# Fused attention and soft-MoE kernel: input loads cut in halves and held to a window of three

## The chip, the cores and the metric

The kernel runs on one core of a Trainium2 chip. The metric is the device time of one execution in microseconds (us); the unchanged kernel was timed three times. One further execution was recorded by the hardware profiler, and everything that is read from a profile or a trace below comes from that one. The core has four compute engines with a queue each (PE for matmuls, DVE for vector work, ACT for activations and copies, POOL for further vector work) and SP, whose queue issues all the DMA transfers of this kernel. Each queue runs its instructions in the order in which they were written.

## The reference

All numbers are 32-bit floats. There are 8 batches of 8 heads, 576 positions and 64 features; `phi` has 32 memory slots per position.

```python
a = softmax(phi, axis=slots)                      # (8, 8, 576, 32); max, exp, sum, divide
k_m = einsum('bhsm,bhsd->bhmd', a, k)             # 576 positions pooled into 32 slots
v_m = einsum('bhsm,bhsd->bhmd', a, v)
attn = softmax(q @ k_m^T / 8, axis=slots)         # (8, 8, 576, 32)
x = (attn @ v_m), heads side by side              # (4608, 512)
logits = x @ moe_phi                              # (4608, 32): 8 experts of 4 slots
d = softmax(logits, axis=rows); slot_in = d^T @ x
slot_out[e] = relu(slot_in[e] @ w1[e]) @ w2[e]    # 8 experts, w1 512x1024, w2 1024x512
out = softmax(logits, axis=slots) @ slot_out      # (4608, 512)
```

The column softmax over all 4608 rows needs every batch, so the experts can only start when the last batch is through.

## The kernel before

**Stages.** For each batch `b` the kernel loads `phi`, `k`, `v` and `q`, pools `k` and `v` over positions (`pool_phi`, `pool_kv`), computes the attention (`attend`) and its share of the routing (`route`). The running parts are merged and end in the tile `SIM` (L1095), the input of all experts. Then the 16 MB of `w1` and 16 MB of `w2` are multiplied in pieces of 1 MB (L1159, L1208), and a last loop forms the 36 output blocks (L1319), copies them out of PSUM by turns on ACT and DVE (L1328, L1330) and stores them (L1338).

**What sets the order.** Nothing is issued where it is written. Every step is handed to a planner (`plan.add`) with its engine, an estimated cost, the tiles that it reads and writes and, for a load, an estimated transfer time. `Plan.order` then plays the whole kernel through with these numbers and emits the steps in the order in which they came out, engine by engine. A step can depend on a part of a tile (`split`, `part`). `FILL` steps (L500) are matmuls on a tile of ones whose result is not used; the planner puts them where PE would be idle.

**Loads.** `load` (L480) is one planner step on SP that issues one DMA. The first loads have fixed places (`FIRST`): `phi0 k0 v0 mphi q0 phi1 k1 v1 q1`. A `phi` load has 576 KB; a `k`, `v` or `q` load has 1152 KB, in four blocks (index `c`) of 128 partitions by 576 numbers. The buffers are few: three for `phi`, two for the pair of `k` and `v`, two for `q`. Weight pieces (`load_w`) lie in the same large tile (`arena`) as the buffers of the attention: six pieces have room of their own, and the others take over space that the attention has given up.

**The steps that the prediction follows, for one batch.** DVE L535 takes the maximum over `phi`; PE L543, DVE L548, PE L557 and ACT L568 spread it; POOL L573 subtracts it, in place in the `phi` tile; ACT L579 is the exponential; POOL L586 adds up; PE L596, DVE L603 and L604 make the reciprocal. PE L623 pools `k` and `v`, ACT L639 and L646 scale them, PE L657 and L658 transpose them, ACT L661 copies the result. DVE L702 transposes `q` in two halves (`q_blocks`: half `h` reads the first or the last two of the four blocks). PE L734 forms scores, twice per batch; DVE L748 transposes them, DVE L765 takes the maximum, POOL L770 subtracts, ACT L775 is the exponential, DVE L780 the sum, DVE L789 its reciprocal, POOL L793 the product, DVE L798 transposes back, PE L809 and ACT L814 turn it for the routing.

Of the kernel before, what the change touches and what calls it, by code (L numbers as in the profile page):

```python
# [16 lines left out]
PE, DVE, ACT, POOL, SP = range(5)  # L17
# [3 lines left out]
class Plan:  # L21
# [19 lines left out]
    def add(self, eng, cost, fn, r=(), w=(), also=(), pri=None, dma=0.0, slack=0.0):  # L41
        i = len(self.ops)
        deps = set()
        tiles = set()
        for x in r:
            for key in x:
                tiles.add(key[0])
                if key in self.last_w:
                    deps.add(self.last_w[key])
        for x in w:  # L50
            for key in x:
                tiles.add(key[0])
# [12 lines left out]
        for t in tiles:  # L65
            t.users += 1
        need = tiles + [t for t in also if t not in tiles]
        self.ops.append((eng, cost, fn, deps, i + self.bias if pri is None else pri, dma, tiles, need, slack))
# [159 lines left out]
def dve(n):  # L228
    return 0.15 + n / 960.0
# [51 lines left out]
def kernel(  # L281
# [24 lines left out]
    nc = tc.nc  # L306
    B, H, S, D = q.shape
# [29 lines left out]
    def keep(name, shape, dtype=F32, parts=1):  # L337
        return Tile(ap=const.tile(shape, dtype, name=name), parts=parts)
# [138 lines left out]

    DMA_RATE = 380e3

    def load(dst, src, nbytes, w, pri=None):  # L480
        add(
            SP, 0.06, lambda: nc.sync.dma_start(dst(), src), w=[w],  # L482
            dma=nbytes / DMA_RATE, pri=pri,
        )


    FIRST = ["phi0", "k0", "v0", "mphi", "q0", "phi1", "k1", "v1", "q1"]
# [1 line left out]
    def first(name):  # L489
        return FIRST.index(name) - 1000 if name in FIRST else None  # L490
# [29 lines left out]
    def rows(x, b):  # L520

        return x[b].rearrange("h (p j) y -> (h p) (j y)", j=J).rearrange("(c r) x -> r c x", r=P)


    def pool_phi(b):
# [1 line left out]
        ph = lambda: pt.ap.rearrange("p (c j m) -> p c j m", c=C, j=J)  # L527
        load(
            lambda: pt.ap.rearrange("p (c x) -> p c x", c=C), rows(phi, b), H * S * M * 4, pt,
            pri=first(f"phi{b}"),  # L530
        )
        mx, mh, mb, es, rs = pmxs.tile(), pmhs.tile(), pmbs.tile(), pess.tile(), prss.tile()
        add(
# [74 lines left out]

    def pool_kv(b, pt, ph, rs):

        kb = kvs.tile().split(2)
        kv = lambda: kb.ap.rearrange("p (i c x) -> p i c x", i=2, c=C)
        for i, (src, name) in enumerate(((k, "k"), (v, "v"))):
            load(lambda i=i: kv()[:, i], rows(src, b), H * S * D * 4, kb.part(i), pri=first(f"{name}{b}"))
        acc = b_kv.tile()
        kp, vm = kps.tile(), vms.tile()

# [64 lines left out]


    def load_q(b):
        qt = qs.tile()
        load(
            lambda: qt.ap.rearrange("p (c x) -> p c x", c=C), rows(q, b), H * S * D * 4, qt,
            pri=first(f"q{b}"),
        )
        return qt  # L690

    def at_view(atb):
# [2 lines left out]
    def q_blocks(qt):  # L695

        halves = []
        for h in range(2):
            qT = qTs.tile()

            def f(h=h, qT=qT):
                nc.vector.transpose(  # L702
                    qT.ap.rearrange("p (i u y) -> p u i y", i=2, y=Y),
                    qt.ap[:, h * QT_SZ: h * QT_SZ + QT_SZ].rearrange("p (u i x) -> p u i x", i=2, x=Y),
                )

            add(DVE, dve(QT_SZ), f, r=[qt], w=[qT])
            halves.append(qT)
        return halves

# [664 lines left out]
```

## Time and profile before

| what | value |
|---|---|
| time, median of 3 runs | 220.69 us (218.91 to 223.28) |
| time of the profiled execution | 219.11 us |
| its span in the trace | 217.3 us |
| granted TensorE clock, mean | 0.954 of full speed |
| busy share PE, DVE, ACT, POOL | 85%, 63%, 39%, 41% |
| moved by DMA | 76.52 MB, 352 GB/s over the span |

The span runs from the first to the last instruction in the trace; 1.81 us of the execution lie outside it. The profiled execution was 1.58 us below the median of the three timed runs. A busy PE here is in part PE on `FILL` matmuls: L500 has 41.0 us of its 184.7 us.

### The profile page before, as it was taken

Reading aid. Unit: us, or ns where it says so; the run is one execution under the profiler, and the core shown is the slowest. Engines: PE = TensorE matmul, PEld = TensorE weight load, DVE = VectorE, ACT = ScalarE, POOL = GpSimd, SP = SyncE. Lnnn points to the kernel's source line nnn. Section 1 sums busy time; section 2 is a strip of 40 time slices with the busy share of each in tenths; the row PEclk is TensorE's granted clock in tenths of the full one; section 3 lists DMA queues with packets and bytes.
Section 4 is the critical chain, followed back from the end, with each engine's and each line's share of the span. In section 5 each row is a group of like instructions: output and inputs, shape, how many; then the busy total and the mean of one; then the engine's idle time right before and its main releaser. Section 6 shows DMA issues by size and latency. Waiting matters only on the chain.

```text
span 217.3 us, 6743 instructions
## 1 busy us (share of the span) xinstructions
PE 184.7 (85%) x2934; PEld 119.5 (55%) x2934; DVE 136.4 (63%) x244; ACT 84.0 (39%) x223; POOL 88.8 (41%) x96
## 2 busy tenths in 40 slices
PE   7698888969699989997999999989999799989700
PEld 7596467556466565655756566566543245644500
DVE  3336495978589798896758787459605840278700
ACT  2022406146066283672563855510103322166600
POOL 3380849486568575869294498000000000000000
PEclk9999999988969999998899999999999999999965
DMA  6999999999999999999944987799999999049997
GB/s 219 383 381 387 382 388 380 389 380 383 359 386 372 391 384 388 344 392 412 403 184 140 416 285 324 250 411 411 407 408 409 407 410 364 16 199 416 416 415 291
DMA packets 27885, 76.52 MB, mean 352 GB/s; under 512 B 1744, under 2 KB 5840, under 8 KB 27856
## 3 DMA queue, kind: packets, MB, share of 16 engines
q1 hardware_dynamic: 27856, 76.09, 92.3%
q8 instruction: 23, 0.38, 0.7%
q14 instruction: 6, 0.05, 0.1%
HBM read 66.65 MB, written 9.44 MB: 350 GB/s over the span
## 4 chain that ended last, share of the span: by engine, by line
PE 48%; DMA 17%; DVE 9%; ACT 8%; issue 6%; POOL 4%; SPq 2%; DVEq 1%; ACTq 0%; POOLq 0%
PE scbank L734 9%; DMA arena<-in_moe_w_dram 9%; PE kvbank L623 8%; PE bank L1159 7%; DMA top<-in_q_dram 5%; PE bank L809 3%; PE bank L912 3%; DMA out_dram<-arena 3%; PE bank L829 3%; ACT arena L579 3%; PE bank L500 2%; PE kvbank L1208 2%; SPq L482 2%; PE bank L934 2%; DVE arena L702 2%
## 5 line engine op out<-in xcount | busy, mean ns | idle before, releaser
L500 PE MATMUL bank<-ones 128*128 128x128 f32 x252 | 41.0, 310 | 1.1 <-DVE ones L445 1.1
L500 PEld LDWEIGHTS bank<-ones 128*128 128x128 f32 x252 | 36.6, 220 | 7.0 <-issue 5.7
L586 POOL TENSOR_TENSOR arena<-arena 128x128 f32<-128x128 f32 (+2 forms) x32 | 23.4, 731 | 12.1 <-ACT arena L579 10.2
L702 DVE STREAM_TRANSPOSE arena<-top 128x1152 f32<-128x1152 f32 x16 | 21.7, 1360 | 9.6 <-DMA top<-in_q_dram 9.6
L573 POOL TENSOR_TENSOR arena<-arena 128x1152 f32<-128x1152 f32 x8 | 21.1, 2632 | 15.8 <-ACT arena L568 15.8
L623 PE MATMUL kvbank<-arena 64*32 64x128 f32 x1152 | 21.9, 279 | 3.3 <-ACT arena L579 1.8
L770 POOL TENSOR_TENSOR arena<-arena,smx 128x576 f32<-128x576 f32 x16 | 18.5, 1158 | 13.6 <-DVE smx L765 13.5
L734 PE MATMUL scbank<-arena 32*32 32x288 f32 x512 | 20.9, 407 | 2.3 <-issue 2.0
L623 PEld LDWEIGHTS kvbank<-arena 64*32 64x32 f32 x1152 | 16.6, 107 | 8.0 <-ACT arena L579 3.6
L748 DVE STREAM_TRANSPOSE arena<-scbank 128x576 f32<-128x576 f32 x16 | 12.4, 777 | 11.8 <-PE scbank L734 11.8
L535 DVE TENSOR_REDUCE arena<-arena 128x128 f32<-128x1152 f32 x8 | 17.5, 2186 | 2.9 <-DMA arena<-in_phi_dram 2.9
L814 ACT COPY arena<-bank 96x384 f32<-96x384 f32 x32 | 14.6, 481 | 11.9 <-PE bank L809 11.9
L793 POOL TENSOR_TENSOR arena<-arena,ssm 128x576 f32<-128x576 f32 x16 | 18.3, 1156 | 1.4 <-DVE ssm L789 1.3
L1208 PE MATMUL kvbank<-arena 128*32 128x512 f32 x128 | 16.0, 600 | 2.7 <-DMA arena<-in_moe_w_dram 2.5
L809 PE MATMUL bank<-ident,arena 128*96 128x128 f32 x96 | 16.2, 294 | 0.7 <-DVE arena L886 0.5
L798 DVE STREAM_TRANSPOSE arena<-arena 128x576 f32<-128x576 f32 x16 | 12.1, 758 | 5.1 <-POOL arena L793 5.1
L1159 PE MATMUL bank<-arena,SIM 128*32 128x256 f32 x256 | 14.2, 380 | 0.7 <-DVE SIM L1095 0.7
L1330 DVE COPY arena<-bank 128x512 f32<-128x512 f32 x18 | 12.1, 690 | 3.8 <-PE bank L1319 3.8
L1319 PE MATMUL bank<-sr,cT 128*128 128x512 f32 x36 | 13.3, 470 | 1.4 <-DVE sr L1306 0.3
L809 PEld LDWEIGHTS bank<-ident,arena 128*96 128x96 f32 x96 | 10.3, 134 | 5.7 <-issue 2.9
L734 PEld LDWEIGHTS scbank<-arena 32*32 32x32 f32 x512 | 8.0, 104 | 8.7 <-issue 3.2
L1328 ACT COPY arena<-bank 128x512 f32<-128x512 f32 x18 | 10.5, 587 | 5.4 <-PE bank L1319 5.2
(113 smaller groups left out, 259.0 us busy)
## 6 DMA issues: line engine op xcount, KB each, us to landing
arena<-in_moe_w_dram SPq DMA_DIRECT2D x32, 1024.0 KB, 11.4
arena<-in_k_dram SPq DMA_DIRECT2D x8, 1152.0 KB, 9.8
arena<-in_v_dram SPq DMA_DIRECT2D x8, 1152.0 KB, 12.5
top<-in_q_dram SPq DMA_DIRECT2D x8, 1152.0 KB, 10.8
out_dram<-arena SPq DMA_DIRECT2D x12, 768.0 KB, 6.8
arena<-in_phi_dram SPq DMA_DIRECT2D x8, 576.0 KB, 11.5
arena<-in_moe_phi_dram SPq DMA_DIRECT2D x1, 64.0 KB, 9.0
```

Of the source, the lines that this page charges most:

```text
L500: lambda: nc.tensor.matmul(warm.ap, ones, ones, start=True, stop=True,),
L535: lambda: nc.vector.tensor_reduce(mx.ap, ph().rearrange("p c j m -> p c m j"), axis=AX.X, op=ALU.max),
L573: lambda: nc.gpsimd.tensor_tensor(ph(), ph(), mb.ap.unsqueeze(2).to_broadcast([P, C, J, M]), op=ALU.subtract),
L586: plus = lambda o, x, y: nc.gpsimd.tensor_tensor(o, x, y, op=ALU.add)
L623: nc.tensor.matmul(acc.ap[M * c: M * c + M, a, : 2 * D], ph()[h0: h0 + HALF, c, j, :], kv()[h0: h0 + HALF, :, c, j * D: j * D + D], start= ...
L702: nc.vector.transpose(qT.ap.rearrange("p (i u y) -> p u i y", i=2, y=Y), qt.ap[:, h * QT_SZ: h * QT_SZ + QT_SZ].rearrange("p (u i x) -> p ...
L734: nc.tensor.matmul(scb.ap[M * c: M * c + M, r, :JY], kT.ap[h0: h0 + Y, i * P + M * c: i * P + M * c + M], qT[c // 2].ap.rearrange("p (i c ...
L770: lambda: nc.gpsimd.tensor_tensor(exv(), exv(), bc(mx), op=ALU.subtract),
L793: lambda: nc.gpsimd.tensor_tensor(exv(), exv(), bc(sm), op=ALU.mult),
L809: nc.tensor.transpose(tp.ap[:T, t * P: t * P + P], aT.ap[:, x: x + T], ident)
L1159: nc.tensor.matmul(hb.ap[NS * j: NS * j + NS, :256], SIM.ap[:, 2 * i + c, NS * e: NS * e + NS], wv[:, c, 256 * j: 256 * j + 256], start=(e ...
L1208: nc.tensor.matmul(pacc.ap[NS * x: NS * x + NS, 0, :DM], hT()[:, 4 * t + 2 * i + j, NS * e: NS * e + NS], wv[:, j, t, :], start=(e == 0 an ...
```

## The change

The loads of `k`, `v` and `q` are cut in two halves of two blocks each (576 KB), and the tiles are split so that a reader can wait for the half that it needs: L702 of half `h` now reads only half `h` of `q`, while L623 still reads all of `k` and `v`. All loads of `phi`, `k`, `v` and `q` are marked `fenced`: before such a load, from the fourth on, SP first issues a DMA that copies four bytes out of the tile filled by the third fenced load ahead of it into a small tile `fence`. The queue has to wait until that load has landed before it can issue the copy, and the load stands behind the copy. The loads of `mphi` and of the weights are not fenced.

```diff
-    def load(dst, src, nbytes, w, pri=None):
-        add(
-            SP, 0.06, lambda: nc.sync.dma_start(dst(), src), w=[w],
-            dma=nbytes / DMA_RATE, pri=pri,
-        )
+    DEPTH = 3
+    fence_b = keep("fence", [1, 8])
+    sent = []
+
+    def load(dst, src, nbytes, w, pri=None, rate=DMA_RATE, fenced=False):
+        def f():
+            if fenced:
+                if len(sent) >= DEPTH:
+                    x = sent[-DEPTH]
+                    k = len(sent) % 8
+                    nc.sync.dma_start(fence_b.ap[:, k: k + 1], x)
+                sent.append(dst()[0:1, 0, 0:1])
+            nc.sync.dma_start(dst(), src)
+
+        add(SP, 0.06, f, w=[w], dma=nbytes / rate, pri=pri)
...
-        kb = kvs.tile().split(2)
+        kb = kvs.tile().split(4)
         kv = lambda: kb.ap.rearrange("p (i c x) -> p i c x", i=2, c=C)
         for i, (src, name) in enumerate(((k, "k"), (v, "v"))):
-            load(lambda i=i: kv()[:, i], rows(src, b), H * S * D * 4, kb.part(i), pri=first(f"{name}{b}"))
+            for h in range(2):
+                x = slice(2 * h, 2 * h + 2)
+                load(
+                    lambda i=i, x=x: kv()[:, i, x], rows(src, b)[:, x], H * S * D * 2,
+                    kb.part(2 * i + h), pri=first(f"{name}{b}"), fenced=True,
+                )
...
-            add(DVE, dve(QT_SZ), f, r=[qt], w=[qT])
+            add(DVE, dve(QT_SZ), f, r=[qt.part(h)], w=[qT])
```

`load_q` is cut in the same way, and the load of `phi` is only marked `fenced`. The planner knows of the halves and not of the copies, and it makes a new order for all engines.

On SP the program began with these loads, in order:

```order
L482 DMA arena<-in_phi_dram 128x4x288
L482 DMA arena<-in_k_dram 128x4x576
L482 DMA arena<-in_v_dram 128x4x576
L482 DMA arena<-in_moe_phi_dram 128x4x32
L482 DMA top<-in_q_dram 128x4x576
L482 DMA arena<-in_phi_dram 128x4x288
L482 DMA arena<-in_k_dram 128x4x576
```

and begins so now (line numbers in rows of the changed kernel are its own; L495 is the load, L493 the copy, `top` holds `q`):

```order
L495 DMA arena<-in_phi_dram 128x4x288
L495 DMA arena<-in_k_dram 128x2x576 x2
L493 DMA fence<-arena 1x1
L495 DMA arena<-in_v_dram 128x2x576
L493 DMA fence<-arena 1x1
L495 DMA arena<-in_v_dram 128x2x576
L495 DMA arena<-in_moe_phi_dram 128x4x32
L493 DMA fence<-arena 1x1
L495 DMA top<-in_q_dram 128x2x576
L493 DMA fence<-arena 1x1
L495 DMA top<-in_q_dram 128x2x576
L493 DMA fence<-arena 1x1
```

The first copy reads `phi0` and stands ahead of the first half of `v0`; from there on a copy stands ahead of each input load.

On DVE, between the scores of batch 0 (`scbank`) and the maximum over `phi2`, before:

```order
L748 STREAM_TRANSPOSE arena<-scbank 128x576
L765 TENSOR_REDUCE smx_79<-arena 128x18
L702 STREAM_TRANSPOSE arena<-top 128x18x2x32
L535 TENSOR_REDUCE arena<-arena 128x128
L748 STREAM_TRANSPOSE arena<-scbank 128x576
L548 TENSOR_REDUCE pmh_83<-bank_63 128x2
L765 TENSOR_REDUCE smx_80<-arena 128x18
```

and now (L768 was L748, L785 was L765, L722 was L702, L548 was L535):

```order
L768 STREAM_TRANSPOSE arena<-scbank 128x576
L785 TENSOR_REDUCE smx_79<-arena 128x18
L722 STREAM_TRANSPOSE arena<-top 128x18x2x32
L768 STREAM_TRANSPOSE arena<-scbank 128x576
L785 TENSOR_REDUCE smx_80<-arena 128x18
L548 TENSOR_REDUCE arena<-arena 128x128
```

The transpose and the maximum of the second scores of batch 0 moved ahead of the maximum over `phi2`.

On PE, where the pooling of batch 7 meets the scores of batch 6, before:

```order
L809 MATMUL bank_64<-ident,arena 96x128 x3
L623 MATMUL kvbank<-arena 32x128 x48
L657 MATMUL bank_62<-ident,arena 128x128 x2
L658 MATMUL bank_62<-ident,arena 128x128
L912 MATMUL bank_64<-arena 32x258 x6
L734 MATMUL scbank<-arena 32x288 x16
```

and now (L829 was L809, L675 was L657, L676 was L658, L684 was L666, L932 was L912, L754 was L734, L641 was L623, L513 was L500):

```order
L829 MATMUL bank_64<-ident,arena 96x128 x3
L675 MATMUL bank_63<-ident,arena 128x128 x2
L676 MATMUL bank_63<-ident,arena 128x128
L684 MATMUL bank_62<-mphd,arena 32x64 x4
L513 MATMUL bank_65<-ones 128x128
L932 MATMUL bank_64<-arena 32x258 x6
L754 MATMUL scbank<-arena 32x288 x16
L641 MATMUL kvbank<-arena 32x128 x24
```

The pooling of batch 7 (L623, now L641) moved from ahead of the transposes and scores of batch 6 to behind them.

More of the change, by code (lines that the diff above doesn't have):

```diff
@@ L529, in pool_phi @@
             lambda: pt.ap.rearrange("p (c x) -> p c x", c=C), rows(phi, b), H * S * M * 4, pt,
-            pri=first(f"phi{b}"),
+            pri=first(f"phi{b}"), fenced=True,
         )
@@ L684, in load_q @@
     def load_q(b):
[L685 to L689, printed above, removed]
+        qt = qs.tile().split(2)
+        for h in range(2):
+            x = slice(2 * h, 2 * h + 2)
+            load(
+                lambda x=x: qt.ap.rearrange("p (c x) -> p c x", c=C)[:, x], rows(q, b)[:, x],
+                H * S * D * 2, qt.part(h), pri=first(f"q{b}"), fenced=True,
+            )
         return qt
```

## Prediction

> **What bounds the kernel now.** The page comes first: the size of the span, the engines, the transfers by slice (40 slices of 5.43 us) and the chain that ended last.
>
> ```profile
> span 217.3 us, 6743 instructions
> DVE  3336495978589798896758787459605840278700
> DMA  6999999999999999999944987799999999049997
> GB/s 219 383 381 387 382 388 380 389 380 383 359 386 372 391 384 388 344 392 412 403 184 140 416 285 324 250 411 411 407 408 409 407 410 364 16 199 416 416 415 291
> PE 48%; DMA 17%; DVE 9%; ACT 8%; issue 6%; POOL 4%; SPq 2%; DVEq 1%; ACTq 0%; POOLq 0%
> ```
>
> No engine is full over the whole span, so the kernel has to be read by stages. The transfers run at about 384 GB/s up to 108 us, then drop, then run at about 410 GB/s to 184 us. To see what ends the stages I took the chain of waits in order of time, and what SP's queue waited for between 86 and 146 us.
>
> ```profile
> 145.05 0.30 DVE SIM L1095
> 145.39 7.98 PE bank L1159 x144
> 167.15 18.83 DMA arena<-in_moe_w_dram
> 186.02 1.06 PE kvbank L1208 x8
> SPq L482 <- PE kvbank L623: 27.6, 3, 11.2
> SPq L482 <- DVE SIM L1095: 3.5, 1, 3.5
> ```
>
> The attention ends with `SIM` at 145.05 us. Behind it everything is fixed: the last weight piece lands at 186 us after an unbroken stream, and its earlier pieces waited for room in the arena, which attention steps (L623, L1095) gave up. So the weight stream and the output loop follow the end of the attention, and whatever moves `SIM` moves the end by as much. The question is what the change does to the 145 us of attention. Here are DVE's rows that touch fresh inputs, from its timeline (start, duration, and in brackets the idle time before and who ended it), and the engines' busy time in four stretches (after the length: PE, PEld, DVE, ACT and POOL, then clock, DMA share and GB/s).
>
> ```profile
> 14.42 2.64 DVE L702 STREAM_TRANSPOSE arena<-top 128x1152 f32<-128x1152 f32 x2 [6.39 <-DMA top<-in_q_dram]
> 16.98 2.10 DVE L535 TENSOR_REDUCE arena<-arena 128x128 f32<-128x1152 f32 x1
> 26.16 1.38 DVE L702 STREAM_TRANSPOSE arena<-top 128x1152 f32<-128x1152 f32 x1 [1.26 <-DMA top<-in_q_dram]
> 28.01 2.15 DVE L535 TENSOR_REDUCE arena<-arena 128x128 f32<-128x1152 f32 x1 [0.47 <-DMA arena<-in_phi_dram]
> 37.09 1.38 DVE L702 STREAM_TRANSPOSE arena<-top 128x1152 f32<-128x1152 f32 x1 [1.99 <-DMA top<-in_q_dram]
> 39.05 2.17 DVE L535 TENSOR_REDUCE arena<-arena 128x128 f32<-128x1152 f32 x1
> 50.57 2.26 DVE L535 TENSOR_REDUCE arena<-arena 128x128 f32<-128x1152 f32 x1
> 92.73 2.23 DVE L535 TENSOR_REDUCE arena<-arena 128x128 f32<-128x1152 f32 x1
> 14.40:40.00 25.60, 21.54 (x564) 16.30 (x570) 17.89 (x23) 7.46 (x19) 16.40 (x17) 1.00 1.06 384
> 60.00:80.00 20.00, 18.83 (x360) 12.45 (x365) 17.58 (x31) 12.04 (x34) 14.29 (x12) 0.91 1.04 382
> 80.00:100.00 20.00, 18.07 (x425) 11.51 (x410) 17.85 (x29) 10.91 (x34) 15.25 (x16) 1.00 1.02 379
> 100.00:118.00 18.00, 17.67 (x388) 11.38 (x385) 11.99 (x23) 8.44 (x26) 10.77 (x10) 0.91 0.69 260
> ```
>
> There are two regimes. Up to 39 us the inputs set the pace: DVE waits for `q0`, `q1`, `phi2` and `q2`. From `q1` (26.16) to `q2` (37.09) seven units of 576 KB arrived (`phi2` one, `k2`, `v2` and `q2` two each) in 10.93 us: 1.56 us a unit, 4.68 us for three. After 39 us no wait of DVE for an input is left. From the fifth L535 (50.57) to the eighth (92.73) a batch takes 14.05 us, while its seven units of input take 10.9, and DVE is busy for 17.58 and 17.85 of 20 us: the compute engines in their written order are the bound, DVE first.
>
> **Part 1, halves of q and the new order on DVE.** With `q` in halves, the transpose of the first half can run about 1.56 us before the second half has landed. For `q0` that lets the second L535 start when `phi1` lands. SP's timeline and the landing of that load say when this is.
>
> ```profile
> 4.57 2.85 SPq L482 DMA_DIRECT2D arena<-in_phi_dram  x1
> DMA to landing us min/median/max: 11.5/11.5/11.5
> ```
>
> That is 4.57 + 11.5 = 16.07 us against 16.98, a gain of 0.91 us, which I cost at nothing: the third L535 waits for `phi2` anyway and takes it back. What lasts is work done in a wait. In the new order L748 and L765 of batch 0's second scores stand ahead of the third L535, and two such rows more than before still stand ahead of the fourth.
>
> ```profile
> L748 DVE STREAM_TRANSPOSE arena<-scbank 128x576 f32<-128x576 f32 x16 | 12.4, 777 | 11.8 <-PE scbank L734 11.8
> L765 DVE TENSOR_REDUCE smx<-arena 128x18 f32<-128x576 f32 x16 | 11.8, 738 | 0.2
> ```
>
> They take 0.78 + 0.74 = **1.5 us** out of waits of 1.26 + 0.47 + 1.99 = 3.72 us. As DVE paces the next stage, I take 1.5 us; bounds 0 (the queue waits later for POOL or PE instead) and 3.7 (all three waits filled). Later the new order does the same work in other places: up to the eighth L535 its list lacks one L780 only. The halves of `k` and `v` bring nothing, since L623 still waits for all four.
>
> **Part 2, the new order on PE.** Near 109 us PE pooled batch 7 before it transposed the keys of batch 6; in the new order the pooling stands behind them.
>
> ```profile
> 108.93 1.59 PE L623 MATMUL kvbank<-arena 64*32 64x128 f32 x96 [0.20 <-ACT arena L579]
> 110.45 0.44 PE L657 MATMUL bank<-ident,arena 128*128 128x128 f32 x2
> 111.93 1.95 PE L734 MATMUL scbank<-arena 32*32 32x288 f32 x32
> ```
>
> The scores of batch 6 (L734, 111.93) can come up to 1.59 us sooner. The pooling is then that much later, and batch 7 depends on it. Between 0 and 1.6 us I take half, **0.8 us**: in this stretch DVE is busy only for 11.99 of 18 us, so this is a chain of latencies in which a step that moves up counts, but two batches share it.
>
> **Part 3, the copies and the window of three.** 48 half loads and 8 `phi` loads make 56 fenced loads, so 53 copies. On SP each costs an issue, 0.43 us in the row of `phi0` below; two issues per unit of 1.56 us fit. No row shows a four-byte DMA in flight, and nobody waits for its landing at once: its `fence` column is used again eight copies later. One step does inherit a wait: POOL L573 overwrites `phi` in place and must let the copy read first.
>
> ```profile
> 0.74 0.43 SPq L482 DMA_DIRECT2D arena<-in_phi_dram  x1
> 28.73 1.56 SPq L482 DMA_DIRECT2D arena<-in_k_dram  x1
> 9.17 2.63 POOL L573 TENSOR_TENSOR arena<-arena 128x1152 f32<-128x1152 f32 x1 [6.81 <-ACT arena L568]
> 44.60 2.62 POOL L573 TENSOR_TENSOR arena<-arena 128x1152 f32<-128x1152 f32 x1
> DMA to landing us min/median/max: 4.3/11.5/16.5
> ```
>
> The copy of `phi3` stands behind both halves of `k3`, whose load went out at 28.73 us, 15.9 us before that batch's L573 at 44.60; the chain through L535 and ACT L568 is the cover, and the cost nothing. For batch 0 the copy goes out at `phi0`'s landing, 0.74 + 4.3 = 5.0 us; even if it took as long as `phi0` itself it would end at 9.7 us, 0.5 us behind 9.17, and that gap closes before `phi2`.
>
> What costs is the window. SP is one queue: while it waits at a copy, every later load, the weights, and in the end the stores stand behind. With three units in flight, a unit lands and lets out a fourth; the cycle of three is one load's way from issue to landing plus the copy's issue. The least crowded 576 KB load is `phi0` with 4.3 us; 4.3 + 0.43 (an issue) is 4.73 us, and with 0.1 us from landing to issue (an estimate from DVE's start at 5.02 after it) 4.8, against the 4.68 that the engines need. So it is almost even: 0.12 us per three units. From 5.0 to 39.05 us there are 7.3 such cycles, **0.9 us** later. Two things bound it. Below: `phi0` includes the start-up from idle engines, and in a running stream the wait may vanish: 0. Above: the trace of the first 40 us has four packets of another kind.
>
> ```profile
> q8 instruction: 23, 0.38, 0.7%
> q8 instruction: 4, 0.07, 0.7%
> ```
>
> The first row is the whole span: 0.7% of 16 engines for 217.3 us is 24.3 us, over 23 packets 1.06 us each, on one engine. Before, a delayed engine fell behind alone while the others ran on through a queue up to 16.5 us deep. Now a unit has landed only when its slowest engine is done, and all 16 wait for it: 4 x 1.06 = 4.2 us at most, 5.1 us with the cycle. I take 0.9, by the nearest row for the cycle, because two units still in flight (3.1 us) cover a delay of 1.06 us. After 39 us a later input costs nothing at first: a batch has 14.05 - 10.9 = 3.1 us to spare.
>
> A rule speaks against the halves. The Trainium skill, "DMA: Bandwidth & Descriptors", section Bandwidth, advises loads of at least 1 MiB for 75% of peak; a half is below that, a whole was above. If each of the nine loads more of batches 0 to 2 paid the 2.0 us that its section "Anatomy of one DMA" gives as fixed, a third of it unhidden, the sum would be 6.0 us worse by this estimate. The same section's fit (2.0 us plus bytes over 436 GB/s) makes 3.35 us of a half load alone, a cycle of 3.8 us, and nothing lost. The trace leans to the second: the stretch from 14.4 to 40 us has 576 KB `phi` loads in it and moves 384 GB/s, though behind a deep queue.
>
> **The sum.** Against the profiled execution: 219.11 - 1.5 - 0.8 + 0.9 = 217.7 us. This execution was 1.58 us below the median of 220.69, so I predict **219.3 us** as a median.
>
> **Rivals.** *Faster: DVE really is the pacer.* All 3.7 us of early waits fill, the PE move gives its full 1.6, and the window costs nothing: 219.11 - 5.3 = 213.8, as a median 215.4 us. For it speaks the 88 to 89% of DVE from 60 to 100 us; against it that the tail after 100 us waits on latencies. *Slower: the window starves the transfers.* If the cycle of three is 5.4 us instead of 4.68, from stalls that all engines share, `phi3` lands 0.7 x 7.3 = 5.1 us late, and no order helps work whose data is not there: 219.11 + 5.1 = 224.2, as a median 225.8 us. It decides from a cycle of about 5.3 us on. The instruction packets speak for it; two units in flight speak against it. *The fence holds nothing back.* If a copy's wait is always over when SP comes to it, because room in the buffers is what SP waits for, there is no window, and halves and order alone act: 219.11 - 2.3 = 216.8, as a median 218.4 us. Against it speaks that `phi` loads were in flight for up to 16.5 us, far longer than three units take.
>
> **How the numbers follow.** Forecast 0.58, faster 0.19, slower 0.16, no window 0.07. A change of less than 2% (4.4 us) can hardly be told from none, since the three runs lie 4.4 us apart. Faster by over 2% means below 216.3, slower above 225.1. The forecast and the rival without a window lie within; nearly all of the faster rival lies below 216.3 and the slower one above 225.1, and some room on each side is for the reordering of the engines, of which I could price two places only: 0.21, 0.61 and 0.18. The range takes in the bounds: 215.4 - 0.9 = 214.5 us, should the 0.91 us of the first part last after all, to 225.8 us.
>
> **What would show it.** Right: SP's rows become pairs of copy and load at about 1.56 us from each other up to 40 us, the DMA row stays at 9 and near 380 GB/s in the first 18 slices; DVE's wait at its first L702 falls from 6.39 by about 1.5 us; the fourth L535 is within 1 us of 39.05; `SIM` comes 1 to 2 us earlier, and the 72 us behind it keep their length. Wrong: GB/s in slices 2 to 8 below 350 would be the window; DVE waits for `q` or `phi` after 45 us too; or an unchanged first 40 us with `SIM` moved by more than 3 us, which would be the new order and not the loads.

## Result: 22 us slower, and the profile after

The changed kernel took **241.99 us** as a median of four runs (241.48 to 243.06), against 219.87 us of before: a ratio of **1.102 [1.096, 1.108]** (in brackets the 95% interval, here and below). The prediction was 219.3 us, with 214.5 to 225.8 as its range. The recorded execution of the changed kernel took 241.48 us. Of four experiments below (e3, e5, e8, e13) the recorded execution was slower than the others of the same kernel, so its trace is read for transfers and for single instructions, and the comparison goes by the others.

The page of the changed kernel, with the rows that were shown of before (a slice is now 5.99 us; `PEclk` is the granted clock in tenths):

```profile
span 239.7 us, 6860 instructions
DVE  4244483786567887924566696754960762058710
PEclk9795579589755999997558999999999999999975
DMA  6999889987998989998999829999999999509997
GB/s 226 289 304 309 296 278 288 308 294 232 304 312 268 334 243 404 310 310 242 300 358 418 345 45 349 415 333 412 414 407 406 411 407 411 212 35 411 410 418 304
PE 38%; DMA 36%; DVE 10%; ACT 6%; SPq 3%; issue 2%; POOL 0%; DVEq 0%; ACTq 0%
```

For the first 20 slices the transfers run mostly near 300 GB/s, where before ran at 384. Later, with the weights alone, they reach 410 as before: the DMA engines can do it, they are not given enough. In the chain that ended last, DMA has 36% instead of 17%: 86 us instead of 37. The stretches, read as before (after the length: PE, its weight loads PEld, DVE, ACT and POOL, then clock, DMA share and GB/s):

```profile
14.40:40.00 25.60, 21.33 (x411) 15.09 (x392) 15.30 (x20) 6.36 (x18) 12.43 (x12) 0.73 0.90 290
60.00:80.00 20.00, 15.13 (x204) 10.17 (x202) 13.83 (x19) 7.36 (x22) 7.23 (x7) 0.66 0.91 291
80.00:100.00 20.00, 17.90 (x465) 11.61 (x461) 16.20 (x30) 8.68 (x27) 14.39 (x16) 1.00 0.94 336
100.00:118.00 18.00, 10.98 (x227) 6.59 (x221) 8.12 (x14) 7.05 (x20) 9.91 (x9) 0.80 0.89 275
```

From 60 to 80 us DVE is busy for 13.83 us where it was 17.58. DVE's timeline tells what it waits for (L722 was L702, L548 was L535, L1115 was L1095):

```profile
14.83 2.82 DVE L722 STREAM_TRANSPOSE arena<-top 128x1152 f32<-128x1152 f32 x2 [7.08 <-DMA top<-in_q_dram]
18.68 2.08 DVE L548 TENSOR_REDUCE arena<-arena 128x128 f32<-128x1152 f32 x1 [1.03 <-DMA arena<-in_phi_dram]
32.73 2.17 DVE L548 TENSOR_REDUCE arena<-arena 128x128 f32<-128x1152 f32 x1 [0.96 <-DMA arena<-in_phi_dram]
47.03 2.22 DVE L548 TENSOR_REDUCE arena<-arena 128x128 f32<-128x1152 f32 x1 [0.60 <-DMA arena<-in_phi_dram]
62.84 2.09 DVE L548 TENSOR_REDUCE arena<-arena 128x128 f32<-128x1152 f32 x1 [4.15 <-DMA arena<-in_phi_dram]
110.87 2.09 DVE L548 TENSOR_REDUCE arena<-arena 128x128 f32<-128x1152 f32 x1 [7.57 <-DMA arena<-in_phi_dram]
167.03 0.29 DVE L1115 TENSOR_TENSOR SIM<-arena,st 128x128 f32<-128x128 f32 x1
```

The maximum over `phi` comes later from batch to batch: the fourth at 47.03 us (before 39.05), the eighth at 110.87 (before 92.73), and each of them waits for its load. `SIM` is at 167.03 us, 21.98 later; 18.14 of these were lost by the eighth maximum and 3.84 behind it. Behind `SIM` stand 72.7 us as before. So the loss lies in the attention.

What holds the loads back is seen in SP's queue and in the chain of waits. First two rows from the lists of waits, one of DVE and one of SP's queue (total, times, longest), then SP's timeline around 20 us, then the steps of the chain that are loads (start, duration from issue to landing):

```profile
DVE arena L548 <- DMA arena<-in_phi_dram: 19.5, 8, 7.6
SPq L493 <- DMA arena<-in_k_dram: 15.2, 15, 5.6
```

```profile
15.46 0.39 SPq L495 DMA_DIRECT2D arena<-in_k_dram  x1
...
20.79 0.59 SPq L493 DMA_DIRECT2D fence<-arena  x1
21.42 0.39 SPq L495 DMA_DIRECT2D arena<-in_v_dram  x1
```

```profile
15.46 5.27 DMA arena<-in_k_dram
21.42 5.33 DMA arena<-in_v_dram
27.44 5.27 DMA arena<-in_phi_dram
...
87.41 10.91 DMA arena<-in_k_dram
```

A half of `k` is issued at 15.46 us and lands 5.27 us later, at 20.73. At 20.79 SP issues the copy that had waited for it; that takes 0.59 us, and at 21.42 the next load goes out. The cycle of three is 21.42 - 15.46 = **5.96 us**, 1.99 us a unit. Without the fence the engines needed 1.56 us a unit. These loads are typical of the stretch from 14.4 to 40 us, where the `k`, `v` and `q` loads took 5.3 to 6.2 us; later ones on the chain took from 4.00 to 10.91.

### The profile page after: what moved, and what is told of

It is laid out like the page before. It is cut to its first block, busy times and chain, and to the rows that moved or that the text cites. A ratio compares the mean times of both kernels' runs of the same rounds, so it can differ in the third digit from the quotient of the medians.

```text
span 239.7 us, 6860 instructions
## 1 busy us (share of the span) xinstructions
PE 194.4 (81%) x2928; PEld 125.6 (52%) x2928; DVE 137.2 (57%) x244; ACT 83.4 (35%) x223; POOL 88.6 (37%) x96
## 4 chain that ended last, share of the span: by engine, by line
PE 38%; DMA 36%; DVE 10%; ACT 6%; SPq 3%; issue 2%; POOL 0%; DVEq 0%; ACTq 0%
DMA arena<-in_k_dram 9%; DMA arena<-in_moe_w_dram 8%; DMA arena<-in_phi_dram 8%; PE scbank L754 6%; PE bank L1179 6%; DMA top<-in_q_dram 5%; DMA arena<-in_v_dram 4%; PE bank L513 4%; PE kvbank L641 4%; PE bank L829 3%; PE bank L932 3%; DMA out_dram<-arena 3%; DVE arena L548 3%; PE bank L849 2%; PE kvbank L1228 2%
## 5 line engine op out<-in xcount | busy, mean ns | idle before, releaser
L513 PE MATMUL bank<-ones 128*128 128x128 f32 x246 | 44.0, 325 | 1.1 <-DVE ones L445 1.1
L513 PEld LDWEIGHTS bank<-ones 128*128 128x128 f32 x246 | 38.0, 229 | 7.7 <-issue 6.2
L754 PE MATMUL scbank<-arena 32*32 32x288 f32 x512 | 25.0, 510 | 9.3 <-DVE arena L768 8.9
L722 DVE STREAM_TRANSPOSE arena<-top 128x1152 f32<-128x1152 f32 x16 | 21.8, 1365 | 13.8 <-DMA top<-in_q_dram 13.7
L586 POOL TENSOR_TENSOR arena<-arena 128x1152 f32<-128x1152 f32 x8 | 21.1, 2632 | 23.1 <-ACT arena L581 18.4
L548 DVE TENSOR_REDUCE arena<-arena 128x128 f32<-128x1152 f32 x8 | 17.1, 2142 | 19.5 <-DMA arena<-in_phi_dram 19.5
L641 PE MATMUL kvbank<-arena 64*32 64x128 f32 x1152 | 23.3, 302 | 0.7 <-ACT arena L592 0.7
L641 PEld LDWEIGHTS kvbank<-arena 64*32 64x32 f32 x1152 | 19.1, 116 | 5.9 <-issue 3.4
L768 DVE STREAM_TRANSPOSE arena<-scbank 128x576 f32<-128x576 f32 x16 | 12.3, 770 | 12.5 <-PE scbank L754 12.4
L754 PEld LDWEIGHTS scbank<-arena 32*32 32x32 f32 x512 | 8.8, 123 | 18.3 <-DVE arena L768 9.4
L834 ACT COPY arena<-bank 96x384 f32<-96x384 f32 x32 | 14.4, 481 | 10.6 <-PE bank L829 10.5
L829 PE MATMUL bank<-ident,arena 128*96 128x128 f32 x96 | 15.9, 295 | 1.5 <-DVE arena L906 0.6
L932 PE MATMUL bank<-arena 96*32 96x258 f32 x96 | 9.4, 418 | 8.5 <-ACT arena L834 6.5
L795 ACT ACTIVATE arena<-arena 128x576 f32<-128x576 f32 x16 | 10.9, 690 | 10.0 <-POOL arena L790 10.0
L829 PEld LDWEIGHTS bank<-ident,arena 128*96 128x96 f32 x96 | 10.8, 137 | 5.2 <-ACT arena L834 2.3
```

The lines of the kernel that those rows point to most:

```text
L513: lambda: nc.tensor.matmul(warm.ap, ones, ones, start=True, stop=True,),
L548: lambda: nc.vector.tensor_reduce(mx.ap, ph().rearrange("p c j m -> p c m j"), axis=AX.X, op=ALU.max),
L586: lambda: nc.gpsimd.tensor_tensor(ph(), ph(), mb.ap.unsqueeze(2).to_broadcast([P, C, J, M]), op=ALU.subtract),
L641: nc.tensor.matmul(acc.ap[M * c: M * c + M, a, : 2 * D], ph()[h0: h0 + HALF, c, j, :], kv()[h0: h0 + HALF, :, c, j * D: j * D + D], start= ...
L722: nc.vector.transpose(qT.ap.rearrange("p (i u y) -> p u i y", i=2, y=Y), qt.ap[:, h * QT_SZ: h * QT_SZ + QT_SZ].rearrange("p (u i x) -> p ...
L754: nc.tensor.matmul(scb.ap[M * c: M * c + M, r, :JY], kT.ap[h0: h0 + Y, i * P + M * c: i * P + M * c + M], qT[c // 2].ap.rearrange("p (i c ...
```

## The experiments

Each ratio is against runs of before on the same chip.

### What the halves, the copies and the new order cost apart

**e4_halves_old_order** is before, with each load of `k`, `v` and `q` issued as two.

```diff
-            SP, 0.06, lambda: nc.sync.dma_start(dst(), src), w=[w],
+            SP, 0.06, lambda: halves(dst(), src, nbytes), w=[w],
...
+        for h in range(2):
+            nc.sync.dma_start(dst[:, 2 * h: 2 * h + 2], src[:, 2 * h: 2 * h + 2])
```

> The kernel before with each k, v and q load issued as two DMAs of 576 KB back to back; planner, order and readers' grouping as before, no copies. Theory W: 218 to 222 us, full transfer rate, no loss from smaller loads. Rival H (a 576 KB load is itself slower than one of 1152 KB, whatever the window): under 350 GB/s between 14.4 and 40 us and 226 us or more. Against e1_no_copies it gives the worth of the new order.

Measured: 221.1 us, ratio 0.998 [0.993, 1.003], `SIM` at 146.38 us. The stretch from 14.4 to 40 us in its trace:

```profile
14.40:40.00 25.60, 21.70 (x593) 16.61 (x575) 16.96 (x23) 7.45 (x19) 16.69 (x16) 1.00 1.06 384
```

Loads of 576 KB cost nothing here, where the queue behind them is deep: 384 GB/s, as with whole loads.

**e1_no_copies** is the changed kernel, halves and new order, without the copies.

```diff
-            if fenced:
+            if False:
                 if len(sent) >= DEPTH:
```

> The changed kernel without the copies: halves and the new order stay, no load waits for another. Theory W (the window of three starves the transfers: 5.27 us from a load's issue to its landing plus 0.69 us until the next load is issued make a cycle of 5.96 us for three units, where the engines need 4.68): 217 to 221 us, 375 GB/s or more between 14.4 and 40 us. Rival O (the new order of the engines is bad by itself): 235 us or more at full transfer rate. Rival C (a copy costs time of its own, window or not): 217 to 221 us too, so this run tells O from the others.

Measured: 227.55 us, ratio 1.027 [1.017, 1.037]. The same stretch in its trace, and then the fourth maximum and `SIM` from DVE's timeline:

```profile
14.40:40.00 25.60, 19.99 (x488) 14.06 (x478) 18.27 (x25) 7.73 (x20) 16.28 (x16) 0.97 1.06 383
```
```profile
39.25 2.16 DVE L548 TENSOR_REDUCE arena<-arena 128x128 f32<-128x1152 f32 x1
153.09 0.29 DVE L1115 TENSOR_TENSOR SIM<-arena,st 128x128 f32<-128x128 f32 x1
```

The transfers are back at 383 GB/s and the fourth maximum is where it was. Without the copies the new order still makes the kernel slower, and it does so late: it is at 39.25 us with the fourth maximum, and 8 us behind at `SIM`. That is above the 217 to 221 us of theory W and far below the 235 of rival O.

**e5_window_old_order** is the counterpart: the order of before on all engines, halves, copies, window of three.

```diff
...
+            n = 2 if nbytes == H * S * D * 4 else 4
+            for c in range(0, 4, n):
+                d = dst()[:, c: c + n]
+                if len(sent) >= DEPTH:
+                    x = sent[-DEPTH]
+                    k = len(sent) % 8
+                    nc.sync.dma_start(fence_b.ap[:, k: k + 1], x)
+                sent.append(d[0:1, 0, 0:1])
+                nc.sync.dma_start(d, src[:, c: c + n])
...
```

> The order of the kernel before on all engines; the loads in halves, with the copies and the window of three. Theory (two losses that add: the window about 16 us, the new order about 5.5 us): the eighth maximum over phi at 107 to 111 us as in the changed kernel, SIM at 160 to 163, time 235 to 238 us. Rival (while inputs are late the order does not matter, the window alone makes all of it): SIM at 166 to 168, 241 to 243 us. Rival (the window is only slow because the new order asks for loads in another sequence): the stretch from 14.4 to 40 us above 340 GB/s and below 228 us.

Measured: 240.09 us, ratio 1.092 [1.086, 1.099]. Again the stretch from 14.4 to 40 us:

```profile
14.40:40.00 25.60, 15.76 (x387) 11.80 (x374) 12.63 (x14) 3.88 (x10) 9.42 (x11) 0.86 0.85 272
```

So **the window of three by itself costs about 20 us** (1.092 of 219.2). The theory and both rivals missed: the two losses do not add (235 to 238), the window does not quite make all of it (241 to 243), and the rate is far below 340. The changed kernel is about 1% above this one, about 2 us, with intervals that overlap: in a starved kernel the new order adds little, if anything.

### What the window limits

The same changed kernel with other depths, and the order of before with whole loads.

```diff
-    DEPTH = 3
+    DEPTH = 4
```

> A copy waits for the fourth load ahead instead of the third; as many copies (52), same order of all other work. Theory W: a cycle of about 6 us now holds four units, 1.5 us each, below the 1.56 us that the engines need, so 219 to 224 us and 360 GB/s or more between 14.4 and 40 us. Rival C (the copy itself takes about 0.45 us of each unit's 2.0, on SP or on a DMA engine): still about 290 GB/s and 238 to 242 us.

e7 has `DEPTH = 2`, e12 `DEPTH = 6`:

> The changed kernel with a window of two (DEPTH = 2). Theory (a load takes about 5.3 us from issue to landing whether two or three are in flight, so the cycle stays near 6 us): 2.9 to 3.1 us a unit, 190 to 205 GB/s from 14.4 to 40 us, the eighth maximum at 155 to 168 us, time 285 to 298 us. Rival (the three share the bandwidth, and two land sooner: 3.4 us and 0.7 for the copy): 2.05 us a unit, 280 GB/s, time 242 to 248 us. Between the two, 2.5 us a unit: about 265 us.

> The changed kernel with DEPTH = 6, 3.5 MB allowed in flight. Theory (something else allows no more than four loads in flight once copies and loads alternate, since the trace of the kernel without copies has about eight and that with DEPTH = 4 has 353 GB/s): 345 to 360 GB/s from 14.4 to 40 us, as with DEPTH = 4. Rival (the number of loads allowed decides): 375 to 384 GB/s, as without copies.

e6 is e5 with whole loads (`n = 4`):

> The order of before, whole loads (k, v, q of 1152 KB, phi of 576 KB), with the copies and a window of three loads: 2.9 to 3.5 MB in flight where the changed kernel has 1.77. Theory (the bytes in flight decide; four halves, 2.36 MB, moved 353 GB/s): 365 to 384 GB/s from 14.4 to 40 us, time 219 to 224 us. Rival (each copy is a stop of the queue that drains the engines, whatever the size): 330 GB/s or less, 230 us or more.

Measured: e2 222.44 us in its recorded execution, 0.8% above before, and 226.11 to 228.50 in the three others (1.028 [1.018, 1.038] for these three); e7 275.05 us, 1.255 [1.247, 1.263]; e12 222.97 us in one run; e6 222.08 us, 1.010 [1.003, 1.017]. The stretch from 14.4 to 40 us of e7 (two), e2 (four), e12 (six) and e6 (three whole loads), in this order, each from the stretches of its own trace:

```profile
14.40:40.00 25.60, 18.02 (x401) 12.61 (x400) 8.72 (x10) 3.73 (x9) 10.12 (x12) 0.73 0.70 213
```
```profile
14.40:40.00 25.60, 20.08 (x498) 14.58 (x505) 17.38 (x23) 7.71 (x20) 16.31 (x17) 0.95 1.02 353
```
```profile
14.40:40.00 25.60, 21.71 (x547) 16.33 (x548) 18.31 (x24) 8.90 (x21) 18.00 (x19) 0.93 1.05 372
```
```profile
14.40:40.00 25.60, 21.80 (x608) 17.04 (x613) 17.02 (x23) 7.46 (x20) 17.56 (x17) 1.00 1.04 365
```

| allowed in flight | GB/s, 14.4 to 40 us | time for that many bytes at that rate |
|---|---|---|
| two halves, 1.18 MB (e7) | 213 | 5.5 us |
| three halves, 1.77 MB (the change) | 290 | 6.1 us |
| four halves, 2.36 MB (e2) | 353 | 6.7 us |
| three whole loads, 2.9 to 3.5 MB (e6) | 365 | 8.1 to 9.7 us |
| six halves, 3.54 MB (e12) | 372 | 9.5 us |
| no fence (e1) | 383 | |

The last column is the bytes over the rate. From two to four halves it grows by 0.6 us a load only, from 5.5 to 6.7, so each load more adds little to the time of a cycle. With few loads in flight the rate is then the bytes in flight over a time that grows slowly. Of the 93 GB/s between three halves and no fence, four halves bring back 63, and 2.9 to 3.5 MB bring back 75 to 82. Two loads of e7's chain of waits, where at most two are in flight, show it (start, and us from issue to landing):

```profile
16.20 4.80 DMA top<-in_q_dram
...
27.28 5.16 DMA arena<-in_v_dram
```

With a third fewer bytes in flight the way to landing is about 5.0 us instead of 5.3. The theory of e7 (a fixed 5.3) put the unit at 3.0 us, the rival (bandwidth shared) at 2.05; it is 589.8 KB over 213 GB/s = 2.77 us, nearer to the theory, while the time of 275 us lies below its 285. e2 is just below the 360 GB/s of its theory and far above the 290 of its rival; the theory of e6 held. My theory of e12, that something else allows four loads only, fell: 372 GB/s. The copy itself is not what costs the rate: with six in flight there are 50 copies instead of 53, two issues a unit as in the changed kernel, and the rate is within 3% of that without any.

e2 and e12 also say something of the new order. All their engines have the order of e1, and their rate is no higher, yet `SIM` comes at 147.83 us in e2's trace and 148.16 in e12's, against 153.09 in e1. So what the new order costs is not a fixed amount.

**e3_weights_behind_inputs** is the changed kernel, in which the weight pieces that go out among the inputs are held until the last input is issued.

```diff
+            if not fenced and nbytes == 1 << 20 and len(sent) < 7 * B:
+                held.append((dst, src))
+                return
...
+            if len(sent) == 7 * B:
+                while held:
+                    d, s = held.pop(0)
+                    nc.sync.dma_start(d(), s)
```

> The changed kernel, with the two weight pieces that SP issues between phi6 and k6 held back until all inputs are issued; window and order of all other engines as they are. Theory W with a second part (an unfenced weight piece inside the window holds up the landing that the copies wait for: k6 took 10.9 us to land behind two pieces, 5.1 us of transfer): 236 to 239 us, the eighth maximum over phi 4 to 6 us earlier than 110.87. Rival (the last batches are late only by what the first forty us lost): 241 to 243 us.

Measured: 239.17 us, ratio 1.074 [1.060, 1.089]. The first stretch, and the eighth maximum from DVE's timeline (L555 here):

```profile
14.40:40.00 25.60, 21.04 (x405) 15.21 (x394) 15.29 (x20) 6.35 (x18) 11.70 (x12) 0.73 0.92 295
```
```profile
108.39 2.16 DVE L555 TENSOR_REDUCE arena<-arena 128x128 f32<-128x1152 f32 x1
```

The eighth maximum comes 2.5 us sooner, where the theory had 4 to 6, and the ratio falls from 1.102 to 1.074. The two weight pieces of 1 MB, not fenced, stand ahead of the fenced load that took 10.91 us to land in the chain of the changed kernel; without them, in e3, no fenced load took longer than 6.4 us. They are a small part of the loss.

**e11_planner_told_290** leaves the window and tells the planner of it.

```diff
-        add(SP, 0.06, f, w=[w], dma=nbytes / rate, pri=pri)
+        add(SP, 0.06, f, w=[w], dma=nbytes / (290e3 if fenced else rate), pri=pri)
```

> The changed kernel, with copies and window of three, but the planner is told 290 GB/s for the fenced loads instead of 380, so that its order and its FILL matmuls expect inputs as late as they are. Theory (the transfers set the end, the order little): the eighth maximum stays at 108 to 113 us, time 238 to 243 us. Rival (an order planned for loads on time is what a window makes expensive): 228 to 235 us.

Measured: 236.53 us, ratio 1.070 [1.046, 1.095]. The stretch from 118 to 146 us, and `SIM` from DVE's timeline:

```profile
118.00:146.00 28.00, 24.80 (x429) 15.90 (x423) 18.92 (x37) 13.71 (x42) 19.53 (x27) 0.94 1.03 410
```
```profile
156.04 0.29 DVE L1115 TENSOR_TENSOR SIM<-arena,st 128x128 f32<-128x128 f32 x1
```

It falls between the two. `SIM` comes at 156.04 us, 11 us before that of the changed kernel, by an order and FILL matmuls that fit late inputs. But only some 5 us of it reach the end: 235.0 - 156.04 = 79.0 us stand behind `SIM` instead of 72.7, and the weight stream runs at 410 GB/s without a gap from 118 to 146 us, so that it had no room left to come sooner. The bandwidth that the window left unused is not had back by this order, which knows of it.

### What the new order costs

Here the steps are issued from a list (no copies, halves): one order up to a step, and the remaining steps in the other order.

```diff
     def order(self):
+        at = {int(i): k for k, i in enumerate(LIST.split())}
...
+            for i in sorted((i for i in ready if i in at), key=at.get):
```

**e8**: the new order up to the seventh maximum over `phi`, then that of before. **e9**: up to the fourth maximum only, which is the part that the prediction's Part 1 spoke of. **e10**: that of before up to the seventh maximum, then the new one, which holds Part 2's place.

> No copies, loads in halves, the new order of all engines up to the seventh maximum over phi, and behind it the remaining steps in the order of before. Theory (the 5 to 6 us of the new order arise behind the seventh maximum, where the chain runs over PE): SIM at 144 to 148 us, time 219 to 222 us. Rival (they are laid up earlier, in the buffers and the clock that the first six batches leave behind): SIM at 151 to 154, time 226 to 229 us.

> No copies, loads in halves, the new order up to the fourth maximum over phi (the part of the new order that the prediction credited with 1.5 us), and behind it the order of before. The run with the new order up to the seventh maximum was 2.7% above before. Theory (that loss arises between the fourth and the seventh maximum, by steps in an order that makes PE stand still and run on at a lower granted clock; the first 39 us are bound by transfers and bring nothing): the fifth maximum at 49 to 51 us, SIM at 144 to 147, time 218.5 to 221.5 us. The prediction's step: 217 to 218. Rival (the early part itself costs it): the fifth maximum at 52 us or later, time 224 to 227 us.

> No copies, loads in halves, the order of before up to the seventh maximum over phi, and from there the remaining steps in the new order (the pooling of batch 7 on PE behind the scores of batch 6, which the prediction credited with 0.8 us). Theory (all the loss of the new order lies ahead of the seventh maximum): 218 to 221 us, SIM at 144 to 147. The prediction's step: 0.8 us less than the halves in the old order, about 218.5. Rival (this part costs as well, as two losses): 223 to 227 us, SIM at 149 to 153.

Measured: e8 225.52 us, ratio 1.027 [1.020, 1.034]; e9 223.91 us, 1.017 [1.006, 1.028]; e10 230.56 us, 1.046 [1.033, 1.059]. Theories of all three fell. The loss is not in one place: each of the three is slower than before, and e10, with the last part alone, is slower than e1 with the whole. A list made of two orders has a seam where they meet, and no run tells what the seam costs, so these three do not give the price of a part of the new order. First e9's third and fourth maximum, from DVE's timeline (L613 here); then rows of e10's chain of waits in order of time, in which L819 is the scores and L578 the FILL matmuls; then PE in a stretch of 3 us in e10 (after the length: busy time, clock, DMA share, GB/s):

```profile
27.95 2.20 DVE L613 TENSOR_REDUCE arena<-arena 128x128 f32<-128x1152 f32 x1 [0.69 <-DMA arena<-in_phi_dram]
39.44 2.18 DVE L613 TENSOR_REDUCE arena<-arena 128x128 f32<-128x1152 f32 x1
```

```profile
81.67 1.13 PE scbank L819 x32
...
99.14 3.48 issue
...
105.07 2.10 PE scbank L819 x32
...
111.85 4.05 PE bank L578 x18
```

```profile
103.00:106.00 3.00, 3.00 (x37) 0.50 1.01 404
```

In e9 the waits of DVE are shorter (0.69 us ahead of the third, none ahead of the fourth; 2.08 and 1.40 in e4), yet both maxima start no sooner (27.70 and 38.93 us in e4): work was moved into a wait and nothing came earlier. In e10 PE stands still for 3.48 us, with nothing that the profile shows to wait for, and then runs at a granted clock of 0.50, busy all the time: the same 32 matmuls of the scores take 2.10 us instead of 1.13. In e1 the pause at that point is 1.50 us, and the clock is 0.50 to 0.71 from 103 to 115 us; in before 1.35 us, and 0.64 to 0.79 for six.

But the same is in e4, which has the order of before and is as fast as before (0.998). Two rows of its chain of waits, in which L741 is the scores, and PE in a stretch of 3 us:

```profile
96.69 1.89 issue
...
101.07 2.10 PE scbank L741 x32
```

```profile
100.00:103.00 3.00, 3.00 (x45) 0.50 1.03 410
```

So a pause of that length with half the clock behind it does not by itself make the kernel slower. One thing the traces show of the pauses without a wait: in before, e1, e4 and e10 one packet of the instruction queue (the packets of 1.06 us in the prediction) starts within 1.2 us of the pause's start, and PE goes on 1.4 to 1.5 us after the packet's end. That PE waits there for its next instructions is likely by this, but no run tests it.

Two more runs were to tell whether this is what the new order loses, and the 3.84 us behind the eighth maximum in the changed kernel too, whose chain of waits there runs over the same operations (L754 the scores, L513 FILL) at the same half clock:

```profile
116.22 2.10 PE scbank L754 x32
...
123.00 4.05 PE bank L513 x18
```

**e13_bridge_the_wait** is the changed kernel, with 24 matmuls on the tile of ones ahead of the step where PE waited for 6.49 us.

```diff
+            seen.append(0)
+            if len(seen) == 4:
+                for _ in range(24):
+                    nc.tensor.matmul(warm.ap, ones, ones, start=True, stop=True)
```

> The changed kernel with 24 more matmuls on the tile of ones (48 in the trace, about 6 us at full clock) on PE right ahead of the fourth L932, where PE waited 6.49 us for the last phi and then ran at a clock of 0.50 from 114 to 127 us. Theory (the starved PE is paid twice, once as the wait and once as half a clock behind it): the clock from 114 to 127 us is above 0.9, the eighth maximum stays at 110 to 112 us, SIM at 161 to 163 instead of 167.0, time 236 to 238.5 us. Rival (the chain behind the wait hangs on latencies of the other engines, or the clock falls all the same): SIM at 165.5 to 168, 240.5 to 243 us.

Measured: 241.29 us, ratio 1.088 [1.078, 1.098]. PE's timeline at the bridge (L934) and behind it:

```profile
113.78 5.62 PE L934 MATMUL bank<-ones 128*128 128x128 f32 x48
...
120.33 1.20 PE L755 MATMUL scbank<-arena 32*32 32x288 f32 x32
...
124.01 2.25 PE L513 MATMUL bank<-ones 128*128 128x128 f32 x18
```

The clock behind the bridge is full, and the scores take 1.20 us, the FILL matmuls 2.25. But in this execution the wait was no longer there: another one, of 2.16 us at 94 us, had put PE on a clock of 0.50 up to 109 us, so that PE was itself late and `phi` had landed when it came to the bridge of 5.62 us; `SIM` is at 167.17 us, as in the changed kernel and as the rival had it. The ratio is lower than that of the changed kernel by a margin that the intervals do not settle. Since the clock was back at full speed before the bridge began, this run does not show what the bridge does for the clock, and what a full clock there is worth stays open.

**e14_new_order_without_nine_fills** is e1 without the nine FILL steps ahead of L849 that took 4.05 us at half clock.

```diff
+                nfill.append(0)
+                if 63 < len(nfill) <= 72:
+                    return
...
```

> The new order, halves, no copies (227.55 us), without the nine FILL steps (18 matmuls in the trace) that took 4.05 us on the chain at a clock of 0.5, ahead of the fifth L849 at 113 us. Theory (these FILL matmuls at half clock are the piece of the new order that costs most): SIM at 148.5 to 151 instead of 153.1, time 222.5 to 225.5 us. Rival (the work behind them waits for other engines, or the clock stays low for longer without them): 226.5 to 229 us.

Measured: 227.85 us, ratio 1.034 [1.027, 1.040]. The step behind them in PE's timeline (L849 there, L853 here):

```profile
111.41 1.50 PE L853 MATMUL bank<-arena 128*32 128x192 f32 x12 [2.05 <-DVE arena L969]
```

The theory fell. The step behind them starts 1.86 us sooner (113.27 in e1) because it now waits for DVE, the clock stays at 0.50, and nothing of it reaches the end: `SIM` is at 152.90 us, in e1 at 153.09.

## Why the prediction was wrong

**The failing step is the cost of the window in Part 3.** Its mechanism, a cycle of three loads that is longer than what the engines need, was named by the step itself and by the rival of a window that starves the transfers, and the runs show it. What failed is its size: 0.9 us forecast, about 20 measured (e5), because the cycle was taken too short and its loss was let end at 39 us. Four terms of it:

- *The way to landing.* I took 4.3 us from `phi0`, "the least crowded" load, and argued that in a running stream it may be less. In the stream of three it was 5.27 to 5.33 on the chain up to 33 us, in the stream of two about 5.0. So it was longer in the running stream than at the start, not shorter.
- *The copy's issue*: 0.43 us forecast, 0.59 measured, and 0.1 us around it. With the first term the cycle is 5.96 us instead of 4.8, against 4.68 needed: 1.28 us of loss a cycle, not 0.12. By the prediction's own 7.3 cycles that makes 9.3 us up to the fourth maximum; measured 8.0.
- *Where it ends.* I let the loss end at 39 us, since a batch had "3.1 us to spare". At 1.99 us a unit the seven units of a batch take 13.9 us, as much as the 14.05 of the compute: the slack was the bandwidth that the window took away. From the fourth to the eighth maximum the changed kernel needs 63.8 us, before 53.7. Four times 13.9 us make 2 of these 10 us, and 2.5 are the two weight pieces (e3). SP issues the `phi` loads of this stretch 15.8, 13.8, 14.4 and 18.6 us apart, the last with the weight pieces between; why the first is longer than 13.9, and the rest of the last, is not shown.
- *The deciding point.* The rival "slower" said it decides from a cycle of 5.3 us on. That was right, and its 5.1 us used the same 7.3 cycles. Its chance of 0.16 was too low, because the only row for the landing (4.3) was a load issued into idle engines; the row for the bytes in flight was there too: up to 16.5 us from issue to landing at 384 GB/s.

**Parts 1 and 2 were credited as gains, and no run shows one.** Together they were to bring 2.3 us; e1, which has both and no window, is 2.7% slower than before. Part 1 credited 1.5 us to two rows moved ahead of DVE's maximum; e9, with the new order up to there, is 1.7% [0.6, 2.8] slower, seam included. It rested on "DVE paces the next stage", read from busy shares. But the chain of waits, quoted at the start of the prediction, had PE 48% and DVE 9%: an engine that is busy while the chain runs over others does not set the pace. Part 2 credited 0.8 us to the pooling of batch 7 on PE; e10, with the part of the order that holds it, is 4.6% slower, seam included. The pause of PE and the clock behind it were in the trace of before (1.35 us, then 0.64) and were not looked at. What the order's cost consists of stays open after e13 and e14: e4 has the same pause and half clock and no loss, and e2 and e12 have the same order and a smaller one.

**Point by point, what should show it.** SP's pairs came about every 2.0 us, not 1.56. The rate below 350 in slices 2 to 8, named as the sign of the window, is 278 to 309. DVE's first L722 waits 7.08 us where 6.39 should have fallen by 1.5. The fourth maximum is 8.0 us late, not within 1. `SIM` is 22 us late, not 1 to 2 us early; the 72 us behind it did keep their length. The sign for the new order, an unchanged first 40 us with `SIM` moved by more than 3, is what e1 shows. That halves by themselves cost nothing was right (e4). POOL's inherited wait for the copy was right as well: in the list of waits its L586 waits for ACT and DVE, never for a DMA.

**The two rules of the Trainium skill**, "DMA: Bandwidth & Descriptors". The page has both from transfers issued from GpSimd, while these go out from SP. The advice of its section Bandwidth, loads of at least 1 MiB, is not borne out behind a deep queue (e4, 384 GB/s); with three loads in flight the whole loads did reach 365 GB/s and the halves 290, but four to six halves came to 353 and 372, so what counted was the bytes in flight. The fit of its section "Anatomy of one DMA" makes 3.35 us of a half load; of the thirty input loads on the chains of e7 and the changed kernel the fastest took 3.80 us, and the cycle of 3.8 us did not come.

## What to carry to other kernels

A queue that waits for landings moves at most the bytes it allows in flight over the time from issue to landing plus reissue; take that time from a load in a stream of the same depth, and allow the bytes that the full rate needs with room (here 2.4 MB gave 353 GB/s, 3.5 MB at most 372, and only a queue without a fence 383), before anything is gated. Slack of compute against transfers is gone once the transfers slow down, so a loss per load has to be counted through to the last load that anyone waits for. A new order of steps is priced in the chain that ended last, not by the busiest engine; and a pause of PE with a low clock behind it is to be looked for in a run that is not slower too, before it is called the cause.

## What was not expected of the hardware

In these traces a pause of PE of a few microseconds was followed by a low clock for some ten: 3.48 us and then 0.50 up to 115 us in e10, 6.49 us and then 0.50 in the changed kernel, 1.50 us and then 0.50 to 0.71 for 12 us in e1, although PE was busy all through these 12 us. The Trainium skill, "TensorE: Matmul & The Clock Gate", section "Part 1: The HAM clock gate", describes a gate with half and full clock which falls after about 3.4 us of idling and rises after about as long of work. The halving agrees (2.10 us against 1.13 for the same matmuls); the durations here do not: in e1 a pause of 1.5 us stood ahead of the fall, and the clock came back after some 12 us of work.

A four-byte copy inside the chip, which nobody waits for, costs SP 0.59 us for its issue, more than the 0.39 us of the 576 KB load behind it.
